# Fast-exponential additions on GpSimd: 64-bit integer additions in place of VectorE's 16-bit ones

## The chip, the cores and the metric

The kernel runs on one core of a Trainium2 chip. A core has five engines with their own instruction queues: TensorE (PE, matmuls), VectorE (DVE), ScalarE (ACT), GpSimd (POOL) and SyncE (SP, here a DMA queue). They share an on-chip memory of 128 partitions (SBUF) and meet by semaphores. Matmuls write to an accumulator memory of eight banks (PSUM). The metric is the device time of one execution in microseconds.

## The reference

One transformer block in bf16 on 2048 tokens of width 640: attention with 32 query heads of width 20 that share one key and one value head, then a gated MLP of width 1536. Layer norm stands ahead of both, and both have a residual.

```python
q = (x @ wq).reshape(B, S, H, Dh)          # transposed to b h s d;  H = 32, Dh = 20
k = x @ wk;  v = x @ wv                    # one head for all queries
p = softmax(einsum("bhqd,bkd->bhqk", q, k) * Dh ** -0.5)
o = einsum("bhqk,bkd->bhqd", p, v)
attention = o.reshape(B, S, H * Dh) @ wo
h  = x + attention(layernorm(x))
h2 = h + (gelu(g) * u) @ w_down            # g, u = layernorm(h) @ w_gate, w_up
```

The softmax needs 32 x 2048 x 2048 exponentials: 2048 tiles of 128 keys by 512 queries.

## The kernel before

**Tiles and packs.** The 32 heads lie in eight groups of four; a head fills 20 of 32 rows of PE. A unit is 512 query columns (one, two or four row tiles, and as many groups as fill the columns) for each of the four heads of a group. For one unit and one tile of 128 keys, four matmuls of 32 rows that run beside each other on PE give four score tiles of 128 x 512, a pack (`issue_qk`, L849; the matmuls L880). 32 units by 16 key tiles are 512 packs, 2048 tiles. A pack takes two pairs of PSUM banks of the three pairs that there are for scores (L800); banks 6 and 7 accumulate the output. The exponentials then run on two engines:

- ScalarE takes tiles in pairs (128 x 1024) or singly, with its exponential (L1212), into `pa` (16 slots).
- VectorE takes the others, the chord tiles, with a fast exponential: `a*score + b`, rounded to 16 bits, is the bit pattern of a bf16 number near the exponential (L1263), in `pd`, slot 0 of three. Two more patterns are that number plus 42 and plus 85, a shift in the exponent's fraction (L1245 in `do_adds`, slots 1 and 2). The three, each with its own weight, add up to a smoother exponential. `pd` has 8 slots of three tiles.

The weighted sum is made by PE: the matmul with the values (PV, L968) runs once for a ScalarE tile and three times for a chord tile, with values that are scaled by `CH_W` (`v_ext`, made on GpSimd, L491, from the unscaled values). A row of ones in `v_ext` gives the softmax's sum. PV matmuls go four at a time, one for each pack row.

**Beside it run** the first layer norm (statistics L367 and L374 on VectorE, the square root as a power on GpSimd, L393, then a reciprocal L397 and the normalisation L435 on VectorE, a DMA transpose on SyncE), the projections, and, as query chunks end, output projection, second layer norm (the same lines again, ten groups of one or two row tiles) and the MLP. All matmuls but QK and PV have line 455. The GeLU (L732, L716) is on ScalarE.

**The order is planned.** While the kernel is built, a planner simulates the five queues with a cost for each operation and, whenever an engine is free, asks what it may do next (`pe_decide`, `act_decide`, `dve_decide`, `pool_decide`, `sp_decide`). What comes out is a fixed order for each queue, with a semaphore wait wherever another engine's result is needed and not known to be done. At run time each engine goes through its queue in that order and cannot step past a wait. So a cost that the planner has wrong shows as a wait.

**The shares.** `issue_qk` sets how many tiles n of a pack go to VectorE: the n with the lowest `max(A + ca, Dv + 900 n)`, where A is the work that ScalarE has in hand, ca what the rest of the pack costs there, and Dv the work in hand on VectorE (`dve_load`, L842):

```python
for n, ca in ((0, 1810.0), (1, 1382.0), (2, 904.0), (3, 478.0), (4, 0.0)):
    m = max(A + ca, Dv + 900.0 * n)
```

Costs are nanoseconds. When a GeLU is waiting, A grows by its cost and 1300. The additions of up to four neighbouring slots become one instruction; `dve_decide` puts them between its other tasks by a priority that rises with the number that are pending (`pend`).

## Time and profile before

| | |
|---|---|
| median of 3 runs (lowest to highest) | 850.53 us (847.38 to 850.93) |
| profiled execution: span on the core | 851.3 us, granted TensorE clock 0.956 |
| PE, DVE, ACT, POOL busy | 730.3, 742.2, 763.4, 26.9 us |
| exponentials on ScalarE (L1212) | 1006 instructions, 722.1 us busy |
| chord tiles on VectorE (L1263) | 520, 355.2 us busy |
| chord additions on VectorE (L1245) | 832, 230.2 us busy |
| POOL pow (L393), POOL value scaling (L491) | 19 and 18 instructions, 12.6 and 6.2 us busy |

The profile is of one execution; its own time is its span, 0.8 us above the median of the runs. Until 20 us the first rows are loaded and normalised, from 24 to 793 us the attention runs with the MLP of earlier rows beside it, and from 801 us on PE alone ends the MLP of the last rows.

An engine's busy time counts instructions that overlap once. A group's line names the source line, the engine, the operation, what it writes and reads, how many there are, then busy us and mean ns of one, then the engine's idle time just before them and what ended it. ScalarE's instructions overlap: their means add up to more than the busy time. The granted clock is the share of full speed that the chip allowed TensorE.

### The profile page before, as it was taken

How to read it: one execution, taken by the hardware profiler on the slowest of the kernel's cores; microseconds unless marked ns; L12 is line 12 of the kernel's file. 1: busy time of each engine (PE TensorE's matmuls, PEld its weight loads, DVE VectorE, ACT ScalarE, POOL GpSimd, SP SyncE). 2: the span in 40 equal slices, each digit the busy share in tenths (PEclk: the TensorE clock that was granted, in tenths of full speed). 3: DMA queues.
4: the chain of work that ended last, by engine and by line, in shares of the span. 5: the costliest groups of instructions: out<-in, count | busy, mean ns of one | idle time of the engine just before them, and what ended most of it. 6: DMA issues, size and time to landing. Idle time of an engine off the chain costs nothing.

```text
span 851.3 us, 17702 instructions
## 1 busy us (share of the span) xinstructions
PE 730.3 (86%) x6973; PEld 269.4 (32%) x6973; DVE 742.2 (87%) x1856; ACT 763.4 (90%) x1070; POOL 26.9 (3%) x60
## 2 busy tenths in 40 slices
PE   0877778778889989999998998999999999898998
PEld 0522222222222222233332222223333333232587
DVE  7768988987898989999999998999999999899533
ACT  0779999999999999999999999999999999999322
POOL 5300000000000000000000000000000000000000
PEclk9969979996898999999999998999999999999999
DMA  6780000100000000000021000000102000000100
GB/s 180 144 283 1 16 2 9 10 1 1 7 12 16 1 2 1 2 1 8 27 31 32 2 1 1 2 1 2 39 2 55 2 2 17 17 9 9 32 17 33
DMA packets 42930, 21.84 MB, mean 26 GB/s; under 512 B 34016, under 2 KB 41568, under 8 KB 42848
## 3 DMA queue, kind: packets, MB, share of 16 engines
q1 hardware_dynamic: 40224, 19.83, 9.6%
q8 instruction: 57, 0.93, 0.5%
q10 hardware_dynamic: 2624, 0.87, 0.5%
q14 instruction: 25, 0.20, 0.1%
HBM read 10.21 MB, written 2.62 MB: 15 GB/s over the span
## 4 chain that ended last, share of the span: by engine, by line
ACT 66%; PE 20%; DVE 10%; DMA 3%; issue 1%; SPq 0%; DVEq 0%
ACT pa L1212 64%; PE ps L455 11%; PE ps L968 5%; PE ps L880 5%; DVE pd L1263 4%; DVE pd L1245 2%; ACT gbuf L732 1%; DMA xn1T<-xn_tmp 1%; DMA xh<-in_A_x_dram 1%; DVE stats L374 1%; DVE stats L367 1%; DMA onT<-onq 0%; DVE xn_tmp L435 0%; DVE xh L646 0%; ACT L1212 0%
## 5 line engine op out<-in xcount | busy, mean ns | idle before, releaser
L1212 ACT ACTIVATE pa<-ps 128x512 bf16<-128x512 f32 (+1 forms) x1006 | 722.1, 935 | 21.4 <-PE ps L880 20.7
L1263 DVE TENSOR_SCALAR pd<-ps 128x512 uint16<-128x512 f32 x520 | 355.2, 687 | 48.4 <-PE ps L880 40.7
L968 PE MATMUL ps<-pd,v_ext 128*32 128x512 bf16 x1560 | 280.3, 405 | 21.3 <-ACT pa L1212 14.1
L968 PE MATMUL ps<-pa,v_ext 128*32 128x512 bf16 x1528 | 272.2, 404 | 11.8 <-ACT pa L1212 8.0
L880 PE MATMUL ps<-qT,kT 32*128 32x512 bf16 x2048 | 211.4, 401 | 53.9 <-ACT pa L1212 26.0
L1245 DVE TENSOR_SCALAR pd<-pd 128x512 uint16<-128x512 uint16 (+2 forms) x832 | 230.2, 319 | 8.8
L880 PEld LDWEIGHTS ps<-qT,kT 32*128 32x128 bf16 x2048 | 57.9, 91 | 229.5 <-DVE pd L1263 195.1
L968 PEld LDWEIGHTS ps<-pd,v_ext 128*32 128x32 bf16 x1560 | 67.2, 95 | 110.1 <-issue 47.9
L968 PEld LDWEIGHTS ps<-pa,v_ext 128*32 128x32 bf16 x1528 | 66.1, 94 | 92.4 <-issue 42.0
L455 PE MATMUL ps<-xn2T,wu_sb 128*128 128x512 bf16 (+2 forms) x360 | 69.0, 317 | 6.0 <-DVE gbuf L747 5.9
L455 PE MATMUL ps<-xn2T,wg_sb 128*128 128x512 bf16 (+2 forms) x360 | 68.1, 311 | 0.0
L455 PE MATMUL ps<-xn1T,wq_pad 128*128 128x128 bf16 (+2 forms) x320 | 47.9, 288 | 21.1 <-DMA xn1T<-xn_tmp 20.3
L455 PE MATMUL ps<-wd_sb,gbuf 128*128 128x320 bf16 x384 | 59.6, 300 | 0.0
L747 DVE TENSOR_TENSOR gbuf<-ps,gbuf 128x512 bf16<-128x512 f32 (+2 forms) x72 | 36.5, 509 | 18.3 <-PE ps L455 11.9
L716 ACT ACTIVATE gbuf<-ps 128x128 bf16<-128x128 f32 (+1 forms) x36 | 11.2, 312 | 38.1 <-PE ps L455 38.1
L455 PEld LDWEIGHTS ps<-wd_sb,gbuf 128*128 128x128 bf16 x384 | 34.3, 98 | 20.9 <-issue 8.1
L455 PEld LDWEIGHTS ps<-xn2T,wu_sb 128*128 128x128 bf16 x360 | 26.6, 99 | 32.3 <-issue 14.3
L393 POOL TENSOR_TENSOR ln_denb<-ln_veb,halfc 128x2 bf16<-128x2 bf16 (+1 forms) x19 | 12.6, 673 | 749.1 <-DVE ln_veb L389 749.1
L455 PEld LDWEIGHTS ps<-xn1T,wq_pad 128*128 128x128 bf16 x320 | 23.2, 103 | 39.8 <-DMA xn1T<-xn_tmp 20.3
L455 PEld LDWEIGHTS ps<-xn2T,wg_sb 128*128 128x128 bf16 x360 | 25.8, 98 | 25.1 <-issue 14.7
L766 DVE TENSOR_TENSOR xh<-xh,ps 128x320 bf16<-128x320 bf16 x32 | 15.4, 482 | 17.4 <-PE ps L455 17.4
L455 PE MATMUL ps<-wo_sb,onT 128*128 128x320 bf16 x160 | 28.3, 301 | 0.1
(47 smaller groups left out, 266.2 us busy)
## 6 DMA issues: line engine op xcount, KB each, us to landing
out_dram<-xh SPq DMA_DIRECT2D x16, 160.0 KB, 1.8
xh<-in_A_x_dram SPq DMA_DIRECT2D x3, 640.0 KB, 9.9
wg_sb<-in_B_w_gate_dram SPq DMA_DIRECT2D x1, 1920.0 KB, 8.9
wu_sb<-in_B_w_up_dram SPq DMA_DIRECT2D x1, 1920.0 KB, 10.2
wd_sb<-in_B_w_down_dram SPq DMA_DIRECT2D x1, 1920.0 KB, 14.0
gbuf<-in_A_wq_dram ACTq DMA_DIRECT2D x2, 400.0 KB, 8.3
wo_sb<-in_A_wo_dram SPq DMA_DIRECT2D x1, 800.0 KB, 5.3
xh<-in_A_x_dram SPq DMA_DIRECT2D x2, 160.0 KB, 2.8
```

The source lines that it names most:

```text
L367: dve(lambda e: e.bn_stats(stats[:, ln, t, 6:12], xh[:, t, HALF:D]), 356, [key], [("st", ln, t, 1)], prio, c)
L374: dve(lambda e: e.bn_stats(stats[:, ln, t, 0:6], xh[:, t, 0:HALF]), 356, [key], [("st", ln, t, 0)], prio, b)
L393: task(("pool",), lambda e: e.tensor_tensor(ln_denb[:, ln, sl], ln_veb[:, ln, sl], halfc[:, 0:n], ALU.pow), 1010, L_POOL, [("veb", kk), "h ...
L455: return lambda e, b: e.matmul(o(b), l, r, start=st, stop=sp, **kw)
L716: task(("act",), lambda e: e.activation(o, bank(bk, n), ACT.Gelu_apprx_tanh), ("gelu", c_act(n)), L_ACT, [("b", bk)], gkeys(b, fc), 1.0, fin2)
L747: dve(lambda e: e.tensor_tensor(o, bank(bk, n), o, ALU.mult), c_dve(n), [("b", bk)] + gkeys(b, fc), gkeys(b, fc), 1.0, fin)
L766: dve(lambda e: e.tensor_tensor(xh[:, t, h * HALF:(h + 1) * HALF], xh[:, t, h * HALF:(h + 1) * HALF], bank(bk, HALF), ALU.add), c_dve(HALF ...
L880: ins = e.matmul(bank(b), kT4[32 * r:32 * r + 32, kt * P:(kt + 1) * P], qT[32 * r:32 * r + 32, s, :], start=True, stop=True, tile_position ...
L968: ins = e.matmul(ps[32 * r:32 * r + 32, ab * 512:(ab + 1) * 512], v_ext[:, it["kt"], it["w"], :], it["ap"], start=st, stop=(j in ends), ti ...
L1212: op = plan.commit("act", lambda e: e.activation(dst, src, ACT.Exp, scale=SM_SCALE), cost, L_ACT, [("b", b0 + i) for i in range(n)], [("pa ...
L1245: op = plan.commit("dve", (lambda w, a: lambda e: e.tensor_scalar(pd[:, w, a], pd[:, 0, a], float(CH_SHIFT[w]), None, ALU.add))(w, a), k * ...
L1263: op = plan.commit("dve", lambda e: e.tensor_scalar(pd[:, 0, s * 512:(s + 1) * 512], bank(b), CH_A, CH_B, ALU.mult, ALU.add), c_dve(512), ...
```

## The change

The two additions of a chord tile move from VectorE to GpSimd. Four neighbouring 16-bit patterns are read as one 64-bit integer; the immediate holds the shift four times (`0x0001000100010001` times 42 or 85), and as no 16-bit sum runs over into the next, each of the four is shifted by itself. A tile of 512 patterns becomes 128 words. At most two neighbouring slots are joined, and only if the second is ready as well. GpSimd takes pending additions ahead of its other tasks. [...]

The planner's prices change with it. VectorE's load no longer counts additions, a chord tile costs it 600 instead of 900 in the choice of n, and a third queue comes in: GpSimd's work in hand, 800 for each tile whose additions are still to come, and 1200 for each tile of the new pack. The lines for additions leave `dve_decide`.

```diff
+    pd64 = pd[:].bitcast(mybir.dt.int64)
...
     def dve_load(t):
         v = max(plan.free["dve"] - t, 0.0)
-        v += sum(600.0 for x in dve_q) + 300.0 * (len(pend) + len(dve_q))
+        v += sum(600.0 for x in dve_q)
...
         nf = pd_free.count(True) - len(dve_q)
+        Pl = max(plan.free["pool"] - t, 0.0) + 800.0 * (len(pend) + len(dve_q))
         best = None
         for n, ca in ((0, 1810.0), (1, 1382.0), (2, 904.0), (3, 478.0), (4, 0.0)):
             if n > nf or (n and state["npack"] < 4):
                 continue
-            m = max(A + ca, Dv + 900.0 * n)
+            m = max(A + ca, Dv + 600.0 * n, Pl + 1200.0 * n)
...
     def do_adds(t):
         k = 1
         s0 = pend[0]["slot"]
-        while k < len(pend) and k < 4 and pend[k]["slot"] == s0 + k:
+        while k < len(pend) and k < 2 and pend[k]["slot"] == s0 + k and pend[k]["at"] <= t + 20:
             k += 1
         recs = pend[:k]
         del pend[:k]
-        fr = {}
         for w in (1, 2):
-            a = slice(s0 * 512, (s0 + k) * 512)
-            op = plan.commit("dve", (lambda w, a: lambda e: e.tensor_scalar(
-                pd[:, w, a], pd[:, 0, a], float(CH_SHIFT[w]), None, ALU.add))(w, a), k * 512 / 3.84 + 60.0, L_DVE,
+            a = slice(s0 * 128, (s0 + k) * 128)
+            sh = CH_SHIFT[w] * 0x0001000100010001
+            op = plan.commit("pool", (lambda w, a, sh: lambda e: e.int64_add(
+                pd64[:, w, a], pd64[:, 0, a], sh))(w, a, sh), k * 128 * 1.7 + 180.0, L_POOL,
                 [("pd", 0, s0 + i) for i in range(k)], [("pd", w, s0 + i) for i in range(k)], at=t)
...
     def dve_decide(t):
...
-        n = len(pend)
-        if n and pend[0]["at"] <= t + 20:
-            pr = 3.0
-            if n >= 2 or t - pend[0]["at"] > 1500 or not opts:
-                pr = 1.2
-            if n >= 4 or pd_free.count(True) < 3:
-                pr = 0.2
-            opts.append((pr, len(opts), None))
...
     def pool_decide(t):
+        if pend and pend[0]["at"] <= t + 20:
+            do_adds(t)
+            return True
         for tk in tasks:
             if tk.engs[0] == "pool" and known(tk) and plan.ready("pool", tk.reads, tk.writes) <= t + 20:
```

More of the change, by code (lines that the diff above doesn't have):

```diff
@@ L1307, in dve_decide @@
         for pr, _, tk in opts:
-            if tk is None:
-                k = 1
-                c = 2 * (min(n, 4) * 512 / 3.84 + 60.0)
-            elif tk.lat is None:
+            if tk.lat is None:
                 c = c_dve(tk.cost)
@@ L1316, in dve_decide @@
                 continue
-            if tk is None:
-                do_adds(t)
-            else:
-                tasks.remove(tk)
-                run_task(t, tk, "dve")
+            tasks.remove(tk)
+            run_task(t, tk, "dve")
             return True
```

## The prediction

> **What bounds the kernel now.** I read the busy shares and the chain first, then the groups by form, then one steady stretch, then who waits for whom, last GpSimd's own timeline. The page's first lines and the head of the chain:

> ```profile
> PE 730.3 (86%) x6973; PEld 269.4 (32%) x6973; DVE 742.2 (87%) x1856; ACT 763.4 (90%) x1070; POOL 26.9 (3%) x60
> ...
> ACT 66%; PE 20%; DVE 10%; DMA 3%; issue 1%; SPq 0%; DVEq 0%
> ```

> Three engines are near 90% and the chain runs mostly over ScalarE. By form (line, engine, operation, shapes, count, busy us, mean ns):

> ```profile
> L1212 ACT ACTIVATE pa<-ps 128x1024 bf16<-128x1024 f32 x522 | 590.4, 1140 | 4.8 <-PE ps L880 4.5 <-PE ps L968 0.2
> L1212 ACT ACTIVATE pa<-ps 128x512 bf16<-128x512 f32 x484 | 345.8, 714 | 16.6 <-PE ps L880 16.1
> ```

> and for VectorE:

> ```profile
> L1263 DVE TENSOR_SCALAR pd<-ps 128x512 uint16<-128x512 f32 x520 | 355.2, 687 | 48.4 <-PE ps L880 40.7
> L1245 DVE TENSOR_SCALAR pd<-pd 128x512 uint16<-128x512 uint16 x650 | 157.8, 285 | 6.1
> L1245 DVE TENSOR_SCALAR pd<-pd 128x1024 uint16<-128x1024 uint16 x166 | 63.1, 422 | 2.7
> ```

> 512 packs of four score tiles gave 522 pairs and 484 singles on ScalarE and 520 chord tiles on VectorE: one tile of each pack goes to VectorE, three to ScalarE. ScalarE's tiles overlap: 722.1 us busy over 522x2+484 = 1528 tiles is 0.473 us a tile, so 1.42 us a pack. A steady stretch (PE, weight loads, VectorE, ScalarE, GpSimd) shows ScalarE full; 144 QK matmuls, 36 packs, start in it, so a pack takes 1.39 us:

> ```profile
> 400.00:450.00 50.00, 46.18 (x454) 16.51 (x451) 47.30 (x124) 49.94 (x71) 0.00 (x0) 1.00 0.15 28
> ```

> VectorE is close behind. The waits say how the two are coupled: QK most often waits for a chord tile to leave its PSUM bank, while few matmuls wait for an addition.

> ```profile
> PEld ps L880 <- DVE pd L1263: 195.1, 421, 1.3
> ...
> PEld ps L968 <- DVE pd L1245: 24.7, 80, 0.5
> ```

> So whatever holds VectorE or PE for longer than the work ScalarE has in hand (about a pack) comes out as idle ScalarE, and so as time. Over 60 to 790 us ScalarE is busy 717.7 of 730 us: 12.3 us is all that a freer VectorE can give without changing the shares.

> **The change part by part.** The sum is made against the profiled execution (span 851.3 us; the runs' median is 850.5, so 0.8 lower).

> *Removed from VectorE:* 832 additions, 230.2 us busy. They stand beside ScalarE, not under it. I book two thirds of the 12.3 us: -8 us (bounds -12 and 0).

> *The shares (L856 to 861).* One tile must wait for GpSimd at 1200 a tile, two at 2400. QK starts when two of three bank pairs are free, so the planner has at most one ScalarE pair, 904, in hand: one tile scores at most 904+1382 = 2286, two at least 2400. Outside GeLU stretches the planner stays at one tile per pack, some 520 tiles; the 1.42 us of ScalarE a pack stay. PV matmuls stay near 2048+2x520. Cost 0. Were the cover wrong, and two tiles common, see the rivals.

> *Added on GpSimd:* two additions of 128 64-bit words a tile, some 1040 instead of 832, hardly ever grouped as tiles come one a pack. No row shows one. The nearest are GpSimd's small tensor_scalars:

> ```profile
> L491 POOL TENSOR_SCALAR v_ext<-v_ext 128x40 bf16<-128x40 bf16 x14 | 4.9, 348 | 22.1 <-DVE v_ext L505 15.5 <-DVE ln_r L397 4.0 <-DVE ln_veb L389 2.0
> ...
> L491 POOL TENSOR_SCALAR v_ext<-v_ext 128x20 bf16<-128x20 bf16 x4 | 1.3, 327 | 0.9 <-ACT v_ext L504 0.7
> ```

> That is 306 ns and 1.05 ns an element: 440 ns for 128 elements, 575 for 256 halves, 880 if every half costs double. I take 575, as a word is two halves. Two make 1.15 us a pack, beside a pack of 1.39 us: hidden, with 0.24 us left; it would bind from 0.70 us each. The eight pd slots hold 8x1.39 = 11 us of tiles, so a later free slot costs nothing. [...]

> *Contention:* at 10.64 us a VectorE cast of two columns took 1.22 us while a GpSimd memset of 1.16 us ran. Some 89 small SBUF operations (L385, L389, L397, L435) may each wait for an addition, at most 89x0.58 = 51 us of VectorE, which has just lost 230. Cost 0, covered by that.

> *What shares GpSimd's queue.* This is where I see the cost. GpSimd also runs pow (L393) and the value scaling (L491), which the additions now surround. The build names the code library of a GpSimd instruction ahead of it when it is not the one named last. Before, one such instruction is in the program, ahead of L787, in a gap of 0.24 us. In the build's list the integer addition stands in other libraries than pow and tensor_scalar, so every change between them must bring a load. Where they stand (start us, us, engine, line):

> ```profile
> 36.54 0.99 POOL L491 TENSOR_SCALAR v_ext<-v_ext 128x40 bf16<-128x40 bf16 x2 [0.22 <-DVE ln_r L397]
> 38.09 0.71 POOL L393 TENSOR_TENSOR ln_denb<-ln_veb,halfc 128x2 bf16<-128x2 bf16 x1 [0.56 <-DVE ln_veb L389]
> 38.88 0.69 POOL L491 TENSOR_SCALAR v_ext<-v_ext 128x40 bf16<-128x40 bf16 x2
> 47.97 0.80 POOL L491 TENSOR_SCALAR v_ext<-v_ext 128x40 bf16<-128x40 bf16 x2 [8.40 <-DVE v_ext L505]
> 53.31 0.82 POOL L491 TENSOR_SCALAR v_ext<-v_ext 128x40 bf16<-128x40 bf16 x2 [4.54 <-DVE v_ext L505]
> 100.42 0.58 POOL L393 TENSOR_TENSOR ln_denb<-ln_veb,halfc 128x1 bf16<-128x1 bf16 x1 [46.29 <-DVE ln_veb L389]
> ```

> The first chord tile is at 34.98 us. After it come four groups in the head (36.5, 38.1, 48.0, 53.3) and nine pows up to 772.8 with additions on both sides: 13 interruptions, two loads each. The tenth pow, 804.9, comes 12 us after the last addition, so its load is covered.

> *What one load costs.* No row shows a change of library. Below stands the 0.24 us at L787; the nearest rows are a table load into ScalarE and, among the DMA issues (KB, us to landing), two transfers of 25 KB:

> ```profile
> L732 ACT ACT_TABLE_LOAD x3 | 3.8, 1283 | 0.1
> ```

> ```profile
> wk_sb<-in_A_wk_dram ACTq DMA_DIRECT2D x1, 25.0 KB, 2.9
> wv_sb<-in_A_wv_dram ACTq DMA_DIRECT2D x1, 25.0 KB, 7.4
> ```

> wk_sb went alone, wv_sb behind 400 KB. [...]

> *What of it reaches the end.* The stretch at 252 us shows both waits:

> ```profile
> 252.13 0.70 POOL L393 TENSOR_TENSOR ln_denb<-ln_veb,halfc 128x2 bf16<-128x2 bf16 x1 [101.28 <-DVE ln_veb L389]
> 252.77 0.49 DVE L1245 TENSOR_SCALAR pd<-pd 128x512 uint16<-128x512 uint16 x2
> ...
> 253.18 0.15 DVE L397 RECIPROCAL ln_r<-ln_denb 128x2 f32<-128x2 bf16 x1
> 253.53 0.69 DVE L1263 TENSOR_SCALAR pd<-ps 128x512 uint16<-128x512 f32 x1 [0.20 <-PE ps L880]
> ```

> First load: the reciprocal has 253.18-252.83 = 0.35 us to spare; behind it in VectorE's queue stands the next chord tile, behind that the next QK. ScalarE has a pack in hand, 1.4 us, so it loses L-1.75. Second load: additions stand still; PE's queue, written for additions at once, halts at the first PV of such a tile, with the next QK behind it, about as far ahead. Again L-1.75. An interruption costs 2L-3.5: at 5.2, 6.9 us, and nine cost 62. In the head, at 7.4, 11.3, and four cost 45. Bounds: L 2.9 gives 2.3x13 = 30, L 7.4 gives 11.3x13 = 147, L 0.24 gives 0.

> Sum: 850.5+62+45-8 = 949.5, so 950 us.

> [...]

> **The rivals.**
> - *Loads cost nothing that matters* (faster). For it: the 0.24 us at L787, and 1.28 for a table, both under the 1.75 us of slack. Against it: at L787 nothing was named before it but, at most, the same library. It decides where L falls below 1.75+4/13 = 2.1 us. Then only the 8 us are left: 842 us (838 to 850).
> - *The shares do move* (faster): VectorE and ScalarE meet where 763.4-0.473x = 512.0+0.683x, at x = 217 more tiles and 661 us, 102 less: 749 us, or 773 with 434 more PV matmuls at four in 0.22 us (24 us) all in the way. Against it: 2400 over 2286.
> - *The addition binds* (slower): at 880 ns, 1.76 us a pack instead of 1.39 over 500 packs is +185: 1035 us without loads. It decides from 0.70 us. Against it: 575 by the nearest row.
> - *Loads eat the gain and no more* (same): L near 2.1, 847 to 855 us.

> **How the numbers follow.** Loads at 2.9 or more: 0.79, their own range 850.5+30-12 = 868 to 850.5+147 = 998. Loads without cost 0.09, shares move 0.02, so faster 0.11. Gain and loads equal 0.04. Addition binds 0.06. Slower is 0.79+0.06 = 0.85. The range runs from 868 to 1025: above 998 it takes in part of the binding addition and loads longer than a row shows, and it leaves out the faster and equal cases (0.15). Half a per cent, 4 us, is what a measurement of this kernel can tell from no change.

> **What the profile after would show.** Right: VectorE without L1245 and busy near 510 us, some 1040 additions on POOL; still some 484 single and 522 paired exponentials; holes of 5 to 8 us on GpSimd before and after each L393, VectorE idle at L397 until POOL L393, PV (L968) waiting for POOL; ScalarE's idle time up by some 100 us, in 13 places. Wrong: additions over 0.7 us apart all along (the addition binds); pows followed at once by additions (no load cost); chord tiles above 600 (shares). The most fragile terms are L and the slack of 1.75 us: a plan that lets PE run further behind the additions would hide the second load.

## The result, and the profile after

The changed kernel takes 1025.51 us (median of 5 runs, 1017.76 to 1027.83), the kernel before 850.53 us in the same comparison (847.38 to 856.99): a ratio of 1.204, 95% interval 1.1975 to 1.2106. The forecast was slower, 950 us, in a range of 868 to 1025: the median stands at its very upper edge. Direction and cause were right; of the 175 us only 99.5 had been worked out. The profiled execution is the fastest of the five, 1017.76 us (span 1015.8; in every run here the time is about 2 us above the span, so the profile before belongs to a run of some 853 us); no profile shows what the others spend beyond it. Ratios and their intervals leave out runs over 1.5% above the fastest of their kernel; only the last two experiments below have such runs, 5 and 2 of 12.

The page's busy shares and its chain:

```profile
span 1015.8 us, 18060 instructions
...
PE 746.2 (73%) x6979; PEld 271.7 (27%) x6979; DVE 552.1 (54%) x1028; ACT 763.9 (75%) x1076; POOL 427.8 (42%) x1100
...
ACT 55%; issue 18%; PE 15%; DVE 7%; POOL 2%; DMA 2%; SPq 0%; POOLq 0%
```

VectorE's busy time fell by 190 us, and GpSimd took on additions of 401 us (the groups below). ScalarE has the same work as before (763.4 us) in a longer span: its idle time grew, not its load. New in the chain is "issue", 18% of it: time in which an engine waits for nothing that the profile names. The groups (line, engine, operation, count, busy us, mean ns, idle us before them and its releaser) say where it lies:

```profile
L1214 ACT ACTIVATE pa<-ps 128x1024 bf16<-128x1024 f32 (+1 forms) x1013 | 723.0, 936 | 182.3 <-PE ps L882 134.2
L1247 POOL INT64_ADD pd<-pd x1040 | 401.3, 398 | 412.0 <-DVE pd L1265 325.7
L1265 DVE TENSOR_SCALAR pd<-ps 128x512 uint16<-128x512 f32 x523 | 358.9, 689 | 274.7 <-PE ps L882 269.1
...
L394 POOL TENSOR_TENSOR ln_denb<-ln_veb,halfc 128x2 bf16<-128x2 bf16 (+1 forms) x19 | 12.6, 672 | 117.3 <-issue 70.4
L398 DVE RECIPROCAL ln_r<-ln_denb 128x2 f32<-128x2 bf16 (+1 forms) x19 | 3.0, 160 | 88.9 <-POOL ln_denb L394 88.9
```

The additions take 398 ns each and the chord tiles are 523, against 520 before. Ahead of its exponentials ScalarE now idles 182.3 us; before it was 4.8 + 16.6 = 21.4. The difference, 160.9 us, is nearly the whole growth of the span (164.5). In the list of waits (us in total, times, longest us) GpSimd stands still ahead of pow (L394), of the value scaling (L492) and of the first addition after each (L1247), and the others wait behind it:

```profile
PEld ps L970 <- POOL pd L1247: 198.9, 262, 13.8
ACT pa L1214 <- PE ps L882: 134.2, 50, 12.7
...
DVE ln_r L398 <- POOL ln_denb L394: 88.9, 11, 26.0
POOL pd L1247 <- issue: 83.6, 14, 6.9
...
POOL ln_denb L394 <- issue: 70.4, 10, 7.6
```

The 14, the 10 and three gaps ahead of L492 (24.3 us) are 13 interruptions of two gaps each, and one gap ahead of the very first addition. They stand where the prediction put them: four in the head (50, 65, 85 and 101 us) and nine pows from 156 to 922 us. The tail's pow, at 996.7, comes 43 us after the last addition and costs nothing. The records of pow's line and of the addition's line in GpSimd's own queue name what happens in the gaps:

```profile
L394 POOLq MODIFY_POOL_CONFIG  x22: 1/11/11, 57.7 to 953.5; - x22
```

```profile
L1247 POOLq MODIFY_POOL_CONFIG  x28: 1/1/11, 35.6 to 923.2; - x28
```

This is read here as the instruction that names a code library, two records for each of 11 and 14 changes (L492 has 6 records for its three; in e9, where the kernel names a library by hand with `load_library`, two stand at that line, L812, with 6.11 us behind them, and none at the additions). It ends in at most 11 ns; the gap behind it, before the next operation (5.75 to 10.13 us), is taken to be the load, which the runs with copies below bear out: in e1 the copies in place of pow have no such record, and the additions have one pair of them with a gap of 7.2 us. One interruption in the timeline (start us, us, engine, line, operation, idle before and its releaser):

```profile
156.29 0.59 POOL L394 TENSOR_TENSOR ln_denb<-ln_veb,halfc 128x1 bf16<-128x1 bf16 x1 [6.96 <-issue]
156.92 0.16 DVE L398 RECIPROCAL ln_r<-ln_denb 128x1 f32<-128x1 bf16 x1 [7.12 <-POOL ln_denb L394]
157.00 0.67 DVE L1265 TENSOR_SCALAR pd<-ps 128x512 uint16<-128x512 f32 x1
...
157.73 0.61 PE L882 MATMUL ps<-qT,kT 32*128 32x512 bf16 x4 [6.94 <-DVE pd L1265]
...
158.39 0.60 ACT L1214 ACTIVATE pa<-ps 128x512 bf16<-128x512 f32 x1 [6.15 <-PE ps L882]
...
162.69 2.26 POOL L1247 INT64_ADD pd<-pd  x6 [5.80 <-issue]
...
163.13 0.61 PE L970 MATMUL ps<-pa,v_ext 128*32 128x512 bf16 x1 [4.79 <-POOL pd L1247]
...
164.56 5.36 ACT L1214 ACTIVATE pa<-ps 128x1024 bf16<-128x1024 f32 x7 [5.57 <-PE ps L970]
```

Read downwards it is the predicted chain. GpSimd loads pow's library (6.96 us), the reciprocal waits, behind it the chord tile, behind that QK, and ScalarE idles 6.15 us. Then GpSimd loads the additions' library (5.80), PE's queue stands at a PV, and ScalarE idles again, 5.57 us. Between the two ScalarE gets one tile of 0.60 us.

Away from the interruptions nothing was lost. The stretch that was shown of the kernel before, and one in the head (columns PE, weight loads, VectorE, ScalarE, GpSimd, then the granted clock):

```profile
60.00:100.00 40.00, 11.49 (x98) 4.00 (x98) 7.47 (x15) 10.48 (x14) 6.60 (x17) 0.57 0.32 107
...
400.00:450.00 50.00, 47.89 (x455) 14.61 (x453) 35.28 (x55) 50.00 (x73) 27.15 (x71) 1.00 0.01 2
```

At 400 to 450 ScalarE is full, PE issues 455 matmuls (454 before) and VectorE fell from 47.3 to 35.3 us. Between 60 and 100 us ScalarE worked 10.5 of 40 us, against 38.3 before.

### The profile page after: what moved, and what is told of

It is laid out like the page before. It is cut to its first block, busy times and chain, and to the rows that moved or that the text cites. A ratio compares the mean times of both kernels' runs of the same rounds, so it can differ in the third digit from the quotient of the medians.

```text
span 1015.8 us, 18060 instructions
## 1 busy us (share of the span) xinstructions
PE 746.2 (73%) x6979; PEld 271.7 (27%) x6979; DVE 552.1 (54%) x1028; ACT 763.9 (75%) x1076; POOL 427.8 (42%) x1100
## 4 chain that ended last, share of the span: by engine, by line
ACT 55%; issue 18%; PE 15%; DVE 7%; POOL 2%; DMA 2%; SPq 0%; POOLq 0%
ACT pa L1214 53%; PE ps L456 6%; PE ps L970 5%; PE ps L882 5%; DVE pd L1265 4%; ACT gbuf L733 2%; POOL pd L1247 1%; DMA xn1T<-xn_tmp 1%; DMA xh<-in_A_x_dram 1%; POOL ln_denb L394 1%; DVE stats L375 1%; DVE stats L368 1%; DVE xn_tmp L436 0%; ACT L1214 0%; ACT L733 0%
## 5 line engine op out<-in xcount | busy, mean ns | idle before, releaser
L1214 ACT ACTIVATE pa<-ps 128x1024 bf16<-128x1024 f32 (+1 forms) x1013 | 723.0, 936 | 182.3 <-PE ps L882 134.2
L1247 POOL INT64_ADD pd<-pd x1040 | 401.3, 398 | 412.0 <-DVE pd L1265 325.7
L1265 DVE TENSOR_SCALAR pd<-ps 128x512 uint16<-128x512 f32 x523 | 358.9, 689 | 274.7 <-PE ps L882 269.1
L970 PE MATMUL ps<-pd,v_ext 128*32 128x512 bf16 x1569 | 286.1, 409 | 95.7 <-POOL pd L1247 66.4
L970 PE MATMUL ps<-pa,v_ext 128*32 128x512 bf16 x1525 | 279.6, 410 | 53.6 <-POOL pd L1247 42.4
L882 PE MATMUL ps<-qT,kT 32*128 32x512 bf16 x2048 | 214.5, 407 | 84.9 <-DVE pd L1265 54.5
L456 PE MATMUL ps<-xn1T,wq_pad 128*128 128x128 bf16 (+2 forms) x320 | 50.6, 302 | 20.1 <-DMA xn1T<-xn_tmp 19.7
L456 PE MATMUL ps<-wd_sb,gbuf 128*128 128x320 bf16 x384 | 62.4, 304 | 0.0
L394 POOL TENSOR_TENSOR ln_denb<-ln_veb,halfc 128x2 bf16<-128x2 bf16 (+1 forms) x19 | 12.6, 672 | 117.3 <-issue 70.4
L398 DVE RECIPROCAL ln_r<-ln_denb 128x2 f32<-128x2 bf16 (+1 forms) x19 | 3.0, 160 | 88.9 <-POOL ln_denb L394 88.9
L456 PEld LDWEIGHTS ps<-wd_sb,gbuf 128*128 128x128 bf16 x384 | 33.9, 98 | 24.3 <-issue 10.7
L456 PE MATMUL ps<-wo_sb,onT 128*128 128x320 bf16 x160 | 31.1, 313 | 3.0 <-DMA onT<-onq 2.0
## 6 DMA issues: line engine op xcount, KB each, us to landing
wd_sb<-in_B_w_down_dram SPq DMA_DIRECT2D x1, 1920.0 KB, 12.3
```

Source lines behind the costliest of these rows:

```text
L394: task(("pool",), lambda e: e.tensor_tensor(ln_denb[:, ln, sl], ln_veb[:, ln, sl], halfc[:, 0:n], ALU.pow), 1010, L_POOL, [("veb", kk), "h ...
L456: return lambda e, b: e.matmul(o(b), l, r, start=st, stop=sp, **kw)
L882: ins = e.matmul(bank(b), kT4[32 * r:32 * r + 32, kt * P:(kt + 1) * P], qT[32 * r:32 * r + 32, s, :], start=True, stop=True, tile_position ...
L970: ins = e.matmul(ps[32 * r:32 * r + 32, ab * 512:(ab + 1) * 512], v_ext[:, it["kt"], it["w"], :], it["ap"], start=st, stop=(j in ends), ti ...
L1214: op = plan.commit("act", lambda e: e.activation(dst, src, ACT.Exp, scale=SM_SCALE), cost, L_ACT, [("b", b0 + i) for i in range(n)], [("pa ...
L1247: op = plan.commit("pool", (lambda w, a, sh: lambda e: e.int64_add(pd64[:, w, a], pd64[:, 0, a], sh))(w, a, sh), k * 128 * 1.7 + 180.0, L_ ...
```

## The experiments

The theory: each change of library is a load of several microseconds, paid wherever somebody waits behind GpSimd's queue. Rivals: a price of the additions themselves or of a share of work that moved; a planner that is wrong about GpSimd's queue in general; and VectorE's relief being worth more or less than the 8 us booked. The kernel before took 851.81 us beside the first four experiments, 850.76 beside the next four and 853.0 beside the last two.

### Take the library changes out of the plan, all or some

e1_copies_both, on the changed kernel (e2_copy_pow has the first half alone, e3_copy_scale the second alone):

```diff
-  lambda e: e.tensor_tensor(ln_denb[:, ln, sl], ln_veb[:, ln, sl], halfc[:, 0:n], ALU.pow),
+  lambda e: e.tensor_copy(ln_denb[:, ln, sl], halfc[:, 0:n]),
...
-  e.tensor_scalar(v_ext[..., w, 0:Dh], v_ext[..., 0, 0:Dh], CH_W[w], None, ALU.mult)
+  e.tensor_copy(v_ext[..., w, 0:Dh], v_ext[..., 0, 0:Dh])
```

> The changed kernel with the pow (L394) and the value scaling (L492) on GpSimd replaced by plain copies at the same places of the same queues, same waits; root and scaling are left out of the computation. A copy needs no code library, so one change of library is left, ahead of the first addition. Theory (loads): each of the 13 interruptions costs (1025.5-842.5)/13 = 14.1 us, so without them about 842.5 plus 6 for the first load: 848 us, within 840 to 860, and the pow's gaps on GpSimd gone. Rival (the additions come too late from a third engine, or wait for it in PE's queue, wherever they stand): nothing changes but the copies, 1000 us or more. Rival (the pow and its reciprocal hold VectorE, load or not): 9 pows times some 6 us stay, about 900 us.

> The changed kernel with the pow alone replaced by a copy (the root is left out of the computation), the value scaling stays a tensor_scalar. Changes of library stay at the scaling: 4 interruptions in the first 110 us and the first load. Theory (loads): 842.5+6+4x14.1 = 905 us, 885 to 925. Rival (it is the pow's own place in VectorE's order): 850 us, as with both replaced.

> The changed kernel with the value scaling alone replaced by a copy (the scaling by the chord weights is left out), the pow stays. One group of pow in the head and nine later interrupt the additions, and the first load stays. Theory (loads): 842.5+6+10x14.1 = 990 us, 965 to 1005. Rival (the head, where transfers run, holds most of the loss): 900 us.

| run | interruptions left | us (lowest to highest) | ratio to before, 95% interval |
|---|---|---|---|
| e1_copies_both | 0 | 861.4 (856.09 to 865.75) | 1.0097, 1.0069 to 1.0126 |
| e2_copy_pow | 4, in the head | 911.6 (909.39 to 914.54) | 1.0697, 1.0638 to 1.0755 |
| e3_copy_scale | 10, the pows | 984.22 (980.64 to 988.27) | 1.1541, 1.1479 to 1.1604 |
| after | 13 | 1025.51 | 1.204, 1.1975 to 1.2106 |

With additions, shares and order as in the changed kernel, 164 of the 175 us are gone once pow and scaling are copies. (e1 still ended just above its expected 840 to 860 us; e2 and e3 came inside theirs.) The price is nearly the same wherever the interruption stands: e2 pays (911.6 - 861.4)/4 = 12.6 us each. For the others one correction is needed. e1 and e2 have something that after and e3 have not, a load at the start of GpSimd's queue, ahead of the identity matrix:

```profile
17.50 0.28 POOL L788 TENSOR_SCALAR_AFFINE_SELECT ident<-ident 128x128 bf16<-128x128 bf16 x1 [7.26 <-issue]
```

Its first QK starts 4.1 us later than that of the kernel before. With those 4.1 us taken off e1, e3 pays (984.2 - 857.3)/10 = 12.7 and the changed kernel (1025.5 - 857.3)/13 = 12.9 each. The execution before it ended in the additions' library here, and with a pow in e3 and after; that this is why the load is there is read from the pattern over the runs (e5 below has it too, and e6, which ends with a pow, has not).

What remains in e1 shows the value of the move without interruptions. The lag of each kernel behind the one before, worked out from the traces as the start of the first QK matmul of a pack minus its start in the kernel before (us):

```
pack (its start before)    e1    e4    e5    e6    e7    e8    e9  after
  0   (23.9)              4.1  -0.4   4.2  -0.6  -3.5  -4.4  -5.5   -0.9
 20   (64.3)              4.6   3.1   3.4  -0.4   4.3   2.7  -3.1   52.4
100  (181.6)              8.6  26.2   4.9  13.1   3.2  13.3   2.3   79.4
300  (477.0)              5.5  38.6  12.9  35.7   1.1  24.5   0.6  111.8
420  (655.6)              1.3  36.3  22.7  53.1   1.0  30.6   0.1  134.6
511  (790.8)             -0.3  45.8  23.5  66.9   2.1  38.5  -1.0  160.7
end  (851.3)              2.9  56.7  23.7  74.0  10.3  35.4   3.3  164.5
```

From pack 100 on, e1 catches up 8.9 us, which is read here as VectorE's relief. It had lost 4.5 between the start and pack 100. The table compares one execution of each kernel, and e1's is the fastest of ten that spread over 9.7 us, so a difference of a few us in it is no more than a hint.

### The same loads on the kernel before, waited for or not

An addition of two words that nobody reads, put into the kernel before at each of the ten pows of the second layer norm. e5_before_behind puts it behind the pow, e6_before_ahead ahead of it, where it waits for the same variance. Both have 20 loads (in e5 the twentieth is at the start).

```diff
+  dum64 = dum[:].bitcast(mybir.dt.int64)
...
+  plan.commit("pool", lambda e: e.int64_add(dum64[:, 2:4], dum64[:, 0:2], 1), 0.0, 0.0,
+              ["dum", ("den", kk)], ["dum2"])      # e6: ahead of pow, with ("veb", kk)
```

> The kernel before (additions on VectorE), and behind each of the ten pows of the second layer norm one integer addition of two words on GpSimd that nobody reads: 20 changes of library, in a queue that is idle otherwise. Theory (a load costs what waits for the queue): GpSimd loads back at once and stands ready for the next pow, so most loads are hidden; only the pows that follow another within 7 and 2 us come late, by some 6.7 and 12.2 us, and 5 and 8 reach the end: 865 us, 852 to 878. Rival (loads hold up the other engines by themselves): 20 x 6 = 120 more, 970 us.

> The kernel before, and ahead of each of these ten pows one such addition that waits for the same variance: the load for the pow now stands between the variance and the root, that for the addition is hidden. Nothing else of GpSimd's is waited for, so this is the first half of an interruption alone. Theory: VectorE waits at the reciprocal for 7 us less its slack, ScalarE loses some 6.2 in nine places, less 9 us of slack, plus 4 for the pair that stands 2 us apart; the tenth is hidden by the last matmuls: 850+56-9+4 = 901 us, 880 to 920. Rival (only the additions' second load costs, ScalarE has work in hand for the first): 865 us, as with the addition behind.

Measured: behind 876.57 us (873.86 to 881.83), ratio 1.0302 (1.0269 to 1.0336); ahead 927.6 us (926.99 to 929.66), ratio 1.0898 (1.0873 to 1.0923). GpSimd's waits of the run with the addition behind:

```profile
POOL dum L401 <- issue: 59.7, 10, 6.5
...
POOL ln_denb L396 <- issue: 14.4, 2, 7.6
POOL ident L793 <- issue: 7.2, 1, 7.2
```

and with it ahead, with VectorE's wait behind it:

```profile
POOL ln_denb L399 <- issue: 70.0, 10, 7.6
```

```profile
DVE ln_r L403 <- POOL ln_denb L399: 62.8, 12, 9.1
```

Additions and their number are out of the question here: VectorE still makes the real ones. Behind the pow, the ten loads to the additions' library and seven of the nine back cost next to nothing, since GpSimd's queue is idle and the back load's instruction is reached at once (the first addition ends at 111.83 us, the first record of a change back stands at 111.8). Of the 23.7 us of lag, 4.2 come from the start load, 1.8 are left for those seventeen, and 6.7 and 11 come from two places where two pows follow each other within 15 us, so that the second pow stands behind a load:

```profile
656.43 0.74 POOL L396 TENSOR_TENSOR ln_denb<-ln_veb,halfc 128x2 bf16<-128x2 bf16 x1 [176.84 <-DVE ln_veb L392]
662.97 0.18 POOL L401 INT64_ADD dum<-dum  x1 [5.79 <-issue]
670.71 0.73 POOL L396 TENSOR_TENSOR ln_denb<-ln_veb,halfc 128x2 bf16<-128x2 bf16 x1 [7.56 <-issue]
```

Ahead of the pow, the same loads cost 74 us: ten waited for, 7.4 each, with gaps of 7.0 us on average. This is a miss, 27 us above the expectation, which had taken slack off each load; none shows. (VectorE, busy for 47.3 of the steady 50 us in the kernel before, has little room there to catch up.) So a load costs what stands behind it: 7.4 us for gaps of 7.0 where VectorE waits, about the whole length, and next to nothing for seventeen in e5.

### Tell the planner

e4_planner_told lets the planner count 6 us for a GpSimd operation whose library is not the last one named:

```diff
+  def plib(which):
+      c = 0.0 if lib[0] == which else 6000.0
+      lib[0] = which
+      return c
...
-  pd64[:, w, a], pd64[:, 0, a], sh))(w, a, sh), k * 128 * 1.7 + 180.0, L_POOL,
+  pd64[:, w, a], pd64[:, 0, a], sh))(w, a, sh), k * 128 * 1.7 + 180.0 + plib(1), L_POOL,
```

> The changed kernel as it is on the chip, but the planner adds 6 us to a GpSimd operation that follows one of the other library, so it places reciprocals, PV matmuls and shares for late results. Every load stays as long as it is. Theory (a load costs only what the fixed order has not provided for): the first half of an interruption is hidden, of the second some 4 us are left for tiles that go to ScalarE instead: 842.5+6+13x4 = 900 us, 870 to 930. Rival (a load by itself holds up the other engines, by memory or a port): order does not matter, 1000 us or more.

Measured 909.4 us (903.78 to 914.17), ratio 1.066 (1.0597 to 1.0723). The loads are as long as before, 5.7 to 7.3 us and once 9.5, yet ScalarE hardly waits. By form:

```profile
L1222 ACT ACTIVATE pa<-ps 128x1024 bf16<-128x1024 f32 x599 | 662.5, 1179 | 14.3 <-PE ps L882 12.0 <-PE ps L970 2.3
L1255 POOL INT64_ADD pd<-pd x862 | 334.5, 400 | 365.9 <-DVE pd L1273 293.2 <-issue 70.5 <-DVE ln_vb L386 1.9
L1222 ACT ACTIVATE pa<-ps 128x512 bf16<-128x512 f32 x413 | 312.5, 757 | 13.7 <-PE ps L882 13.5
L1273 DVE TENSOR_SCALAR pd<-ps 128x512 uint16<-128x512 f32 x437 | 299.1, 689 | 243.0 <-PE ps L882 236.8
```

ScalarE's idle time fell from 182.3 to 14.3 + 13.7 = 28.0 us. The cover has a price: the plan keeps tiles off the chord path while a load is due, 437 chord tiles instead of 523, and 86 x 0.473 = 41 us more on ScalarE by that estimate; its exponentials are busy for 758.5 us in place of 722.1 in the kernel before. So the interruption is not a fixed cost; 12.8 us is what it costs in a queue order made without it.

### Keep the additions on GpSimd and bring no load into the stretch

e7_no_load makes the inverse root on VectorE, ten small instructions from a bit pattern and two refining steps, scales the values on VectorE, and names the additions' library ahead of the identity. e8_shares_moved is e7 with prices that send more tiles down the chord path.

```diff
-  task(("pool",), lambda e: e.tensor_tensor(ln_denb[:, ln, sl], ln_veb[:, ln, sl], halfc[:, 0:n], ALU.pow),
+  steps = [
+      lambda e: e.tensor_single_scalar(yb.bitcast(U16), ln_veb[:, ln, sl].bitcast(U16), 1, ALU.logical_shift_right),
+      lambda e: e.tensor_scalar(yb.bitcast(U16), yb.bitcast(U16), -1.0, 24375.0, ALU.mult, ALU.add),
+      lambda e: e.tensor_tensor(a, yb, yb, ALU.mult),
...
-  task(("pool",), (lambda w: lambda e: e.tensor_scalar(
+  task(("dve",), (lambda w: lambda e: e.tensor_scalar(
...
-  Pl = max(plan.free["pool"] - t, 0.0) + 800.0 * (len(pend) + len(dve_q))        # e8 only
+  Pl = max(plan.free["pool"] - t, 0.0) + 400.0 * (len(pend) + len(dve_q))
-  m = max(A + ca, Dv + 600.0 * n, Pl + 1200.0 * n)
+  m = max(A + ca, Dv + 690.0 * n, Pl + 700.0 * n)
```

> The changed kernel without any change of library: the inverse root on VectorE (a bit pattern as first guess, two Newton steps, ten small instructions a group), the value scaling on VectorE, and the additions' library named once, ahead of the identity, so that neither the start nor the first addition loads. Theory: with the pow and scaling as copies it was 861.4 us, of which the load at the start moved the first QK by 4.1 us and the first addition's load held ScalarE some 6 us; without both 851 us, 842 to 856, the 9 us of gain in the steady part included. Rival (the 26 more small VectorE operations per two groups, or GpSimd as third engine, cost more than they give): 865 us or more.

> The kernel without loads, with GpSimd's price in the choice of n lowered from 1200 to 700 a tile (backlog from 800 to 400) and VectorE's raised from 600 to 690, so that many packs give two tiles to VectorE. Rival of the prediction (the shares move and balance ScalarE and VectorE): 100 us less ScalarE, 750 to 790 us. Theory (a pack with two chord tiles holds a bank pair for 0.45+2x0.69+0.25 = 2.1 us, longer than a pack of 1.39 us, so QK waits for VectorE instead): no gain, 850 to 900 us, with ScalarE's busy share down and QK's waits for L1265-type chord tiles up.

e7: 866.19 us (861.7 to 868.39), ratio 1.0165 (1.0139 to 1.0192); a miss, 15 us above the expectation. With no load at all it is slower than the kernel before. The table has it within 2.1 us of that kernel from pack 300 on; it loses 7.8 us between the start and pack 20, where VectorE is full with the small instructions (17.0 of 17.0 us between 23 and 40, 12.7 before), and 8.2 after the last pack. That end is a matter of the planned order more than of the ten instructions, which take 1.9 us there (841.65 to 843.53): the last output projection and normalisation stand at 834 to 846 us, and PE, busy for 3.6 of these 12.6 us, waits for them. In the kernel before they lie at 797 to 809 us with 40 us of matmuls still to do.

e8: 888.18 us (885.72 to 890.94), ratio 1.0431 (1.0398 to 1.0463); the shares did move, and it is slower than e7. By form:

```profile
L1284 DVE TENSOR_SCALAR pd<-ps 128x512 uint16<-128x512 f32 x710 | 468.8, 685 | 161.6 <-PE ps L901 158.9
L989 PE MATMUL ps<-pd,v_ext 128*32 128x512 bf16 x2130 | 315.8, 397 | 17.8 <-ACT pa L1233 6.8 <-DVE pd L1284 6.6 <-issue 1.1
L989 PE MATMUL ps<-pa,v_ext 128*32 128x512 bf16 x1338 | 278.5, 400 | 6.4 <-ACT pa L1233 4.2 <-DVE pd L1284 1.4 <-POOL pd L1266 0.4
```

710 chord tiles need 2130 PV matmuls, so there are 3468 in all against 1572 + 1524 = 3096 in e7. ScalarE has 71 us less to do than in e7 (649.9 against 720.5) and idles 126.9 us for QK, where e7 idles 28.7. The steady 50 us of e8:

```profile
400.00:450.00 50.00, 45.87 (x455) 15.87 (x454) 37.52 (x63) 43.95 (x57) 35.72 (x94) 1.00 0.15 28
```

ScalarE is no longer full there (50.0 in e7), but PE issues the same number of matmuls in the kernel before, e7 and e8 (454, 455, 455), and a tile that leaves ScalarE gives it two more of them to do. So PE looks like the next bound; that is read from the equal counts and was not tested. The expectation had another reason, that QK would wait longer for chord tiles. Its sign did not come: these waits are 123.1 us in e8 and 189.7 in e7.

### Hide the loads where GpSimd's queue is idle

e9_hidden_loads follows from e5: one refining step instead of two, pow kept on GpSimd for the last group alone (43 us after the last addition), the identity moved behind the weight copies, so that the change of library ends before the first addition. e10_hidden_more_chord differs in a price.

```diff
+  if ln == 1 and tiles[0] == 15:
+      task(("pool",), lambda e: e.tensor_tensor(ln_denb[:, ln, sl], ln_veb[:, ln, sl], halfc[:, 0:n], ALU.pow),
...
+  lambda e: e.tensor_scalar(a, a, -0.5, 1.50088, ALU.mult, ALU.add),
+  lambda e: e.tensor_tensor(ln_r[:, ln, sl], a, yb, ALU.mult),
...
-  Pl = max(plan.free["pool"] - t, 0.0) + 800.0 * (len(pend) + len(dve_q))        # e10 only
+  Pl = max(plan.free["pool"] - t, 0.0) + 400.0 * (len(pend) + len(dve_q))
```

> The additions stay on GpSimd, and both changes of its code library are put where its queue is idle: the inverse roots of the first nine groups and the ones-column scalings run on VectorE (six small instructions a group, one refining step), the root of the last group stays on GpSimd behind the last addition, and the identity is built behind the weight copies, so that the change to the additions' library lies ahead of the first addition. Theory (what is left when no change of library is waited for is the relief of VectorE): no load is met on the path, the lag behind the kernel before grows by 0 to 6 us in the head, where VectorE gets the small instructions, falls by about 9 us from the 100th pack to the 511th, as it did in the run with copies on GpSimd, and the tail costs nothing: 842 us, 836 to 852. Rival 1 (the head and the tail cost what they did in the run with all roots on VectorE, where VectorE was over 75% busy in the head): 855 to 866. Rival 2 (a load still stands on the path at the start or ahead of the last normalisation): +4 to +7 us on the theory's time, and a gap of 6 to 7.6 us on GpSimd with a waiting VectorE or ScalarE behind it.

> As the run with hidden loads, with GpSimd's prices in the choice of a pack's exits lowered (1200 to 1000 ns a tile, 800 to 400 ns for each tile in the queue), so that somewhat more tiles go through the chord path, fewer than in the run in which 710 did. Theory A (ScalarE is the bound in the steady stretch, 50.0 of 50 us busy, and TensorE at 46 has room): each tile moved takes 0.47 us from ScalarE, and the time falls by 2 to 8 us against the run with hidden loads. Theory B (TensorE is the bound as soon as tiles are moved, because a chord tile takes three PV matmuls and a tile of ScalarE one): the time rises, by up to 22 us x (tiles moved)/186, as from 524 to 710 tiles it rose by 22 us.

e9: 859.83 us over all twelve runs (848.35 to 864.44), ratio 1.0044 (1.0009 to 1.0079) to the kernel before, so no faster (profiled span 854.6 us). The theory's 842 us did not come; the first rival's price did. GpSimd shows the loads where they were meant to be, the first in its idle queue and the other, whose records stand at 791.8 us, ahead of the last pow, which waited for its variance until 836.1:

```profile
21.80 0.28 POOL L812 TENSOR_SCALAR_AFFINE_SELECT ident<-ident 128x128 bf16<-128x128 bf16 x1 [6.11 <-issue]
```

```profile
POOL ln_denb L397 <- DVE ln_veb L392: 44.3, 1, 44.3
```

So it is not the loads that hold it. It starts 5.5 us ahead, loses 7.8 by pack 100, gains 3.3 up to the last pack and loses 4.3 in the tail. In the tail the last normalisation again comes late: PE waits for its transpose with 12 us of matmuls behind it, while in the kernel before PE works through from 800.9 us on. The ends of the two chains, e9 and before:

```profile
837.41 2.45 DMA xn2T<-xn_tmp
839.91 11.94 PE ps L477 x144
```

```profile
800.89 47.61 PE ps L455 x514
```

In the head two things differ from the kernel before and were not taken apart: VectorE is full again between 23 and 40 us, and the granted clock is 0.75 there against 0.97.

e10 ran with the backlog price lowered alone; the 1200 a tile that its expectation names as lowered too stayed. That moved almost nothing, 526 chord tiles against 524. It took 856.81 us (850.54 to 865.85), ratio 1.0053 (1.0025 to 1.008). On the question it was meant for, a few more chord tiles, it says nothing. None of the versions tried beats the kernel before.

## Why the prediction was right, and where it was short

**Shares, additions, VectorE.** Right: 523 chord tiles, 522 paired and 484 single exponentials became 512 and 501. The additions were put at 575 ns and measured 398, 0.77 us a pair beside a pack of 1.39, so the term stays at nothing and the rival of a binding addition falls. Contention at nothing fits the steady stretch, full as before. VectorE is busy for 552.1 us, not near 510: its instructions overlap (the groups' busy times add up to 806.2 us before, the engine's is 742.2), so that taking out 230.2 us of additions freed 190.1. The 512.0 in the sum of the rival with moved shares has the same fault. The 880 ns of the binding addition are twice 440; with every half at double price it would be 306 + 256 x 2.1 = 844 ns.

**Relief of VectorE, -8 us.** e1 shows 8.9 from pack 100 on; e9 shows 3.3 and e7 1.1, with small instructions added on VectorE. It is a few microseconds, and 8 is near its top; single executions do not tell it more closely.

**Number and place of the interruptions.** Right: 13, and the tail's hidden. Not foreseen was the load ahead of the first addition (6.87 us); in e1 its lag of 10.1 us at pack 10 is down to 4.6 at pack 20.

**What one load costs.** The prediction's L, the length of a load, was the author's estimate from two DMA transfers of 25 KB (2.9 and 7.4 us): midway, 5.2 us, in the quiet stretches, and 7.4 in the head, where the DMA share was 1.03 before (40 to 60 us). No run shows a load of 5.2 us, nor that a load's length goes by such transfers. The 13 gaps to pow or scaling are 6.65 to 7.64 us and once 10.13, on average 7.3; the 13 back are 5.75 to 6.20, on average 5.9. The direction makes a difference, and so, it seems, does the place: the 10.13 and the 6.87 us ahead of the first addition fell where transfers ran (DMA share 0.66 and 0.95), as did the longest gaps of e2 and e4, 9.5 us each (0.92 and 1.04). So the higher L in the head had something in it, but that was not tested, and most of the head's loads are no longer than the later ones. With the slack as predicted, these lengths make 13 x (7.3 + 5.9 - 3.5) = 126 us instead of 107: 19 of the missing time.

**What of it reaches the end.** This step failed: "Second load ... about as far ahead. Again L-1.75." The L-1.75 of the first load failed as well. ScalarE's idle time grew by 160.9 us, 12.4 an interruption, of 13.2 us of gaps: 0.8 us of slack in place of 3.5, worth (3.5 - 0.8) x 13 = 35 us. The timeline shows why. ScalarE had more in hand than the sum gave it: it works on for 2.9 us after the first load begins (149.33 to 152.24). But when the load ends, the way back to it, by pow, reciprocal, chord tile and QK, takes 2.1 us (156.29 to 158.39), and the sum has no term for that way; 2.9 - 2.1 leaves 0.8 of slack, and of 6.96 us of gap 6.15 reach ScalarE. The second load begins 0.6 us after the first ends, when a single tile has been passed on. ScalarE runs dry 2.1 us later, the way back takes 1.9 us, and of 5.80 us of gap 5.57 reach it. The other late interruptions are alike: over the nine, ScalarE stands still for 10.8 to 12.7 us of gaps of 12.5 to 13.5 us, that is 0.4 to 2.0 us of slack for both loads together.

The sum as measured on the profiled execution: 851.3 + 160.9 of idle ScalarE + 3.8 between the last pack and the end is 1016.0, against a span of 1015.8. The relief is inside the 160.9 us already. So the profiled growth of 164.5 us is the forecast's 99, plus 19 for longer loads, 35 for slack, 8 for a relief that was counted apart and 4 after the last pack. The other 10.5 of the 175 us lie between the profiled executions and the medians, and no profile shows them.

**The range.** By its own bounds the loads reached 998 us. The measured time meets the edge of the range (1025.5 against 1025; 1.204 x 850.5 is 1024) only because the range ran on to 1025 for part of a binding addition, which did not come, and for loads longer than the rows' 7.4 us, of which there were few. The miss came from the slack, which had been named as fragile in the other direction only, and from loads nearer to the upper bound than to the middle. That the edge lay just there is luck.

**The rivals.** Loads that cost nothing, or that only eat the gain: 12.8 us each. Shares that move to the good, 749 to 773 us: in after they stayed, and in e8, where they moved, the time rose; the rival's sum had PE's additional PV matmuls as 24 us at most, and left out that PE may be the next bound.

## What to carry to other kernels

Before an operation is moved to an engine that looks idle, list what else goes through that engine's queue in the same stretch, and what stands between two of a kind: here 18 small instructions, worth 10 us of work, cost 168 us by being of another kind than the 1040 additions around them. A load was worth about its length where an engine waited behind it (7.4 us each in e6) and next to nothing in an idle queue (1.8 us for seventeen in e5), so ask of each who is next behind it; and when you count what the busiest engine has in hand, take off the way back to it after the stall. And measure the gain with the stall taken out before building around the stall: with every interruption gone, the move was worth at most some 9 us of 850, and each way of removing the loads gave it back.

## What was not expected

- **A loaded library seems to outlast the execution.** Kernels whose GpSimd queue ends in the additions' library and begins with the other have a gap of 7.2 to 7.3 us ahead of the identity (e1, e2, e5), and their first QK is 3.8 to 4.2 us later; those that end with a pow do not (after, e3, e4, e6). This is a pattern over the runs; no run was made to test it.
- **The two directions differ:** 5.75 to 6.20 us to the additions, 6.65 to 7.64 (once 10.13) to pow or scaling, in the changed kernel's 13 interruptions. Why was not tried.
- **The clock fell with the holes.** The mean granted clock is 0.877 against 0.956; between 146 and 172 us, around the interruption shown, it was 0.62, against 1.00 in the kernel before, and the four QK matmuls right after the hole took 0.61 us where 0.39 is usual. What this adds to an interruption was not separated from the loads.
